# Moving one remainder's transposes from the matrix engine to DMA, four casts from ACT to GpSimd, and loading one weight in four pieces

## The chip, the cores and the metric

One core of one Trainium2 chip. The metric is the device time of one execution in microseconds (us), the median of several. The kernel before takes 534.5 us. The granted clock of PE is given as a share of full speed (1.00).

Names: PE is TensorE's matmuls, PEld its weight loads, DVE is VectorE, ACT ScalarE, POOL GpSimd, SP SyncE. A cast here is a copy from float32 to bf16.

## The reference

Eight batches of retention (attention with a decay and no softmax), whose output is the input of a mixture of four experts. The mixing weights are given, so every token goes through every expert.

```python
def _attn_ref(q, k, v):                      # q, k, v: (8, 8, 576, 64) float32
    scores = scale * np.matmul(q, k.transpose(0, 1, 3, 2))
    Dmat = np.where(rel >= 0, gamma ** rel, 0.0)
    return np.matmul(scores * Dmat, v)

def _moe_ref(x, domain_probs, w1, w2):       # x: (4608, 512), 4 experts, 1024 hidden
    p = domain_probs / (domain_probs.sum(-1, keepdims=True) + 1e-09)
    for e in range(E):
        h = np.maximum(x @ w1[e], 0.0)
        out += p[:, e:e + 1] * (h @ w2[e])
```

## The kernel before

The kernel works in bf16 through 9 token tiles of 512 tokens. Its order of instructions is fixed by hand. A batch has 576 tokens: 512 in blocks and a **remainder** of 64 whose queries go against the last 128 keys (class `Rem`). Retention work is put between expert matmuls by numbered **slots**: after each group of up or down products, `run(slots, n)` issues what hangs at slot `n`. The first token tile has slots 0 to 31, eight for each expert (four up groups, four down groups), so 16 to 19 are the up groups of the third expert (number 2) and 20 to 23 its down groups.

```python
    class Rem:
        def cast(self, engine=nc.gpsimd): ...          # k, q scaled by decays to bf16; v to bf16
        def trans_pe(self):
            pt = ring_tile("ptr", [128, 2, NP, 128], BF16)          # PSUM, one of 4 in turn
            for i, n, w in ((0, "k", 128), (1, "q", R)):
                for p in range(NP):
                    nc.tensor.transpose(pt[:, i, p, 0:w], bfr[n]..., ident[0:w, 0:w])
            nc.scalar.activation(self.kT, pt[:, 0], Copy)
            nc.scalar.activation(self.qT, pt[:, 1, :, 0:R], Copy)
        def trans_dma(self):                                        # used by later batches
            for dst, n, w in ((self.kT, "k", 128), (self.qT, "q", R)):
                nc.sync.dma_start_transpose(out=dst, in_=bfr[n]...)
        def scores(self):
            ...4 matmuls sr <- kTr, qTr
            nc.vector.tensor_tensor(self.sT, s, trir..., op=MULT)   # "the mask"
        def values(self):
            ...8 matmuls or <- sTr, bfr_v and or <- qTr, sbd; then ACT copies to xt

    def w_sum(which, lo, hi): ...      # sums of down weights, 128x1024 each, on DVE

    class Unit:                        # a quarter of batch 0 or 1 (two heads' halves)
        def cast(self, n, engine):
            if n == "v":
                if engine is nc.scalar: nc.scalar.activation(dst, self.raw["v"], Copy)
                else:                   engine.tensor_copy(dst, self.raw["v"])
                return
            engine.tensor_tensor(dst, self.raw[n], ..., op=MULT)

    load_w1_at = {1: (slice(0, F // 4),), 2: (slice(F // 4, F // 2), slice(F // 2, F))}
    ...
    load_w1(2); load_w2(2); load_v(0); load_v(1); load_w1(3); load_v(2); load_w2(3)  # GpSimd's DMA queue
    ...
    remainder(slots, 0, (-1, 13, 15, 16, 17))    # cast 13, transposes 15, scores 16, values 17
    def v_cast(u):
        vs[u].cast("k", nc.vector); vs[u].cast("q", nc.vector); vs[u].cast("v", nc.scalar)
        ...
    # for units 0 to 3 of batch 1: slots of cast, transposes, scores, values
    for u, (c, tr, sc, o) in enumerate(((17, 20, 22, 23), (19, 22, 24, 25), (24, 0, 28, 29), (25, 0, 29, 30))): ...
    for j, ats in enumerate(((18, 18, 19, 20), (20, 21, 23, 23), (28, 28, 29, 29), (30, 30, 40, 41))): ...  # w_sum
```

Each engine works through its own list in order: where DVE's list says "cast unit 0's k, then ..., then the mask", a late k holds up the mask.

## Time and profile before

| | before |
|---|---|
| time, first series | 534.53 us (534.08 to 535.23, 6 runs) |
| span of the profiled run, mean granted clock | 533.0 us, 0.999 |
| PE busy, PE instructions | 523.9 us (98%), 4220 |

This is DVE's timeline of the kernel before (columns: start, length, engine, line, operation, output<-inputs, shapes, count, and in brackets the idle time before it with what ended it):

```profile
48.41 0.42 DVE L338 TENSOR_TENSOR sTr<-sr,trir 128x256 bf16<-128x256 f32 x1 [0.98 <-PE sr L337]
49.82 0.69 DVE L529 TENSOR_TENSOR bf_k<-raw_k,gk 128x512 bf16<-128x512 f32 x1 [0.99 <-DMA raw_k<-in_k_dram]
...
57.72 1.41 DVE L409 SCALAR_TENSOR_TENSOR acc<-po,pm,acc 128x512 f32<-128x512 f32 x2 [1.78 <-PE po L397]
```

`sTr` is the mask of the remainder: it comes ahead of the casts of batch 1's unit 0, which wait for a DMA until 49.82. `acc` is the accumulation that empties a PSUM buffer; DVE is 1.78 us early for it.

### The profile page before, as it was taken

Reading aid. Unit: us, or ns where it says so; the run is one execution under the profiler, and the core shown is the slowest. Engines: PE = TensorE matmul, PEld = TensorE weight load, DVE = VectorE, ACT = ScalarE, POOL = GpSimd, SP = SyncE. Lnnn points to the kernel's source line nnn. Section 1 sums busy time; section 2 is a strip of 40 time slices with the busy share of each in tenths; the row PEclk is TensorE's granted clock in tenths of the full one; section 3 lists DMA queues with packets and bytes.
Section 4 is the critical chain, followed back from the end, with each engine's and each line's share of the span. In section 5 each row is a group of like instructions: output and inputs, shape, how many; then the busy total and the mean of one; then the engine's idle time right before and its main releaser. Section 6 shows DMA issues by size and latency. Waiting matters only on the chain.

```text
span 533.0 us, 10194 instructions
## 1 busy us (share of the span) xinstructions
PE 523.9 (98%) x4220; PEld 342.1 (64%) x4259; DVE 361.4 (68%) x458; ACT 85.2 (16%) x173; POOL 147.8 (28%) x191
## 2 busy tenths in 40 slices
PE   8999999999999999999999999999999999999997
PEld 4644544478745885478646865587548844884486
DVE  6436768895577667697678757776765567557763
ACT  4723440012101111020101101110110000000010
POOL 5744104245244434235232604053000000000000
PEclk9999999999999999999999999999999999999999
DMA  9999947878769866837363675454011111110001
GB/s 242 187 216 245 249 131 189 171 153 170 174 147 154 165 140 152 161 77 171 98 137 92 147 134 115 104 122 123 20 41 29 52 39 41 41 42 19 1 24 56
DMA packets 145054, 63.55 MB, mean 119 GB/s; under 512 B 123760, under 2 KB 135808, under 8 KB 145008
## 3 DMA queue, kind: packets, MB, share of 16 engines
q1 hardware_dynamic: 134080, 43.42, 36.8%
q0 software_dynamic: 10784, 19.35, 16.9%
q8 instruction: 33, 0.54, 0.4%
q10 hardware_dynamic: 144, 0.13, 0.1%
q14 instruction: 13, 0.11, 0.1%
HBM read 53.56 MB, written 9.51 MB: 118 GB/s over the span
## 4 chain that ended last, share of the span: by engine, by line
PE 73%; ACT 2%; issue 0%; DVE 0%
PE ph L358 36%; PE pd L474 34%; ACT xt L291 2%; PE o L283 1%; PE o L278 1%; PE py L474 1%; DVE h L364 0%; PE or L343 0%; PE sr L337 0%; PE or L345 0%; DVE ob L502 0%
## 5 line engine op out<-in xcount | busy, mean ns | idle before, releaser
L358 PE MATMUL ph<-xt,w 128*128 128x512 bf16 x1102 | 248.8, 379 | 2.5 <-DVE h L364 0.2
L364 DVE SCALAR_TENSOR_TENSOR h<-ph,pB 128x1024 bf16<-128x1024 f32 x128 | 156.5, 1224 | 57.5 <-PE ph L358 56.6
L358 PEld LDWEIGHTS <-w 128*128 128x128 bf16 x1136 | 109.9, 98 | 127.9
L474 PEld LDWEIGHTS <-h 128*128 128x128 bf16 x1024 | 99.9, 98 | 13.4
L474 PEld LDWEIGHTS <-s 128*128 128x128 bf16 x768 | 75.0, 98 | 8.7
L474 PE MATMUL pd<-wx,h 128*128 128x256 bf16 x512 | 61.1, 273 | 0.2
L474 PE MATMUL pd<-wx,s 128*128 128x256 bf16 x512 | 61.1, 273 | 0.0
L219 POOL DMA_DIRECT2D pB<-pd x28 | 15.8, 565 | 151.3 <-DVE h L364 151.3
L509 POOL TENSOR_TENSOR ob<-v,p 128x256 f32<-128x256 f32 x15 | 11.3, 756 | 115.8 <-DVE v L506 86.4
L238 POOL TENSOR_TENSOR bf_k<-raw_k,gk 128x512 bf16<-128x512 f32 x24 | 26.6, 1108 | 35.0 <-DMA raw_k<-in_k_dram 17.1
L270 DVE TENSOR_TENSOR sT<-s,tri 128x1024 bf16<-128x1024 f32 x24 | 28.3, 1219 | 6.4 <-PE s L268 6.4
L291 ACT ACTIVATE xt<-o 128x768 bf16<-128x768 f32 (+6 forms) x24 | 13.0, 594 | 116.8 <-PE o L283 116.8
L447 DVE TENSOR_TENSOR s<-s,h 128x1024 bf16<-128x1024 bf16 x32 | 31.5, 1024 | 0.0
L474 PE MATMUL pd<-t4w,h 128*128 128x256 bf16 x256 | 30.6, 273 | 0.0
L397 PE MATMUL po<-wx,h 128*128 128x512 bf16 x124 | 28.6, 379 | 0.3 <-issue 0.2
L474 PE MATMUL pd<-t3w,h 128*128 128x256 bf16 x240 | 28.7, 273 | 0.0
L474 PE MATMUL pd<-t2w,s 128*128 128x256 bf16 x240 | 28.7, 273 | 0.0
L482 ACT ACTIVATE p<-pd 128x256 f32<-128x256 f32 x16 | 6.1, 384 | 138.5 <-PE pd L474 112.8
L238 POOL TENSOR_TENSOR bf_q<-raw_q,gq 128x512 bf16<-128x512 f32 x24 | 27.3, 1138 | 1.9 <-DMA raw_q<-in_q_dram 1.8
L451 DVE TENSOR_TENSOR s<-h,s 128x1024 bf16<-128x1024 bf16 x32 | 24.3, 799 | 0.0
L445 DVE TENSOR_TENSOR s<-h 128x1024 bf16<-128x1024 bf16 x32 | 24.1, 794 | 0.0
L491 DVE TENSOR_TENSOR u<-pd,p 128x256 f32<-128x256 f32 x15 | 6.4, 425 | 22.9 <-PE pd L474 22.9
(161 smaller groups left out, 375.5 us busy)
## 6 DMA issues: line engine op xcount, KB each, us to landing
pB<-pd POOLq DMA_DIRECT2D x28, 256.0 KB, 3.7
raw_k<-in_k_dram SPq DMA_DIRECT2D x48, 128.0 KB, 2.7
raw_q<-in_q_dram SPq DMA_DIRECT2D x48, 128.0 KB, 2.9
raw_v<-in_v_dram SPq DMA_DIRECT2D x48, 128.0 KB, 3.0
out_dram<-oa SPq DMA_DIRECT2D x16, 256.0 KB, 2.4
out_dram<-ob SPq DMA_DIRECT2D x15, 256.0 KB, 2.2
w<-in_moe_w_dram POOLq DMA_DIRECT2D x3, 1024.0 KB, 14.0
wx<-in_moe_w_dram POOLq DMA_DIRECT2D x3, 1024.0 KB, 14.9
```

The lines of the kernel that those rows point to most:

```text
L219: eng.dma_start(out=pB[t, e], in_=pd[e:e + 1, t * NT:(t + 1) * NT].to_broadcast([128, NT]))
L238: eng.tensor_tensor(bfs[p % 2][n], raw1[n], g[:, :, 2 * p:2 * p + 2].unsqueeze(3).to_broadcast([128, NC, 2, D]), op=MULT)
L270: nc.vector.tensor_tensor(sT[:, :, :, :].rearrange("p j c t -> p (j c) t"), s[:, :, :, :].rearrange("p j c t -> p (j c) t"), tri[:, :].uns ...
L291: nc.scalar.activation(xt_of(t)[:, self.ps, n0 + a - t * NT:n0 + z - t * NT], o[:, :, a:z], Copy)
L358: nc.tensor.matmul(ph[:, f, :], lhsT=w1_sb[e][:, dc, fc * 128:(fc + 1) * 128], rhs=x[:, dc, :], start=(dc == 0), stop=(dc == NDC - 1))
L364: nc.vector.scalar_tensor_tensor(h[:, fk:fk + 2, :], ph, 0.0, pB[t, e][:, :].unsqueeze(1).to_broadcast([128, 2, NT]), op0=MAX, op1=MULT)
L397: nc.tensor.matmul(po[:, gg, :], lhsT=h[:, e * NFC + fc, (2 * m + gg) * 128:(2 * m + gg + 1) * 128], rhs=wx[e // 2][:, (e % 2) * NFC + fc, ...
L445: nc.vector.tensor_tensor(self.alloc("s1")[:, l], h[:, l, self.b], h[:, r, self.b], op=ADD)
L447: nc.vector.tensor_tensor(self.alloc("s2")[:, l], self.s1[:, l], h[:, l, self.a], op=SUB)
L451: nc.vector.tensor_tensor(self.alloc("s4")[:, l], h[:, r, self.a], self.s2[:, l], op=SUB)
L474: mm = nc.tensor.matmul(dst, lhsT=src[:, kk, tok], rhs=rhs(c), start=(start and c == 0), stop=(c == KH - 1), skip_group_check=True)
L509: nc.gpsimd.tensor_tensor(self.ob[:, HF:Dm], self.v, self.p5, op=ADD)
```

## The change

Intent: give PE's eight transposes of batch 0's remainder to DMA, whose result is needed only some 13 us after the remainder's inputs are there; take four casts from ACT; and let the first expert's last up weights arrive in smaller pieces. To give the DMA transposes time, the remainder's products move from slots 16 and 17 to 19 and 20, and the casts of units 0 and 1 one slot on. That puts the mask behind unit 0's casts and two weight sums in DVE's list.

```diff
-        def trans_pe(self): ...              # the eight transposes on PE and two copies on ACT
         def cast(self, n, engine):
             if n == "v":
-                if engine is nc.scalar:
-                    nc.scalar.activation(dst, self.raw["v"], Copy)
-                else:
-                    engine.tensor_copy(dst, self.raw["v"])
+                engine.tensor_copy(dst, self.raw["v"])
                 return
-    load_w1_at = {1: (slice(0, F // 4),), 2: (slice(F // 4, F // 2), slice(F // 2, F))}
+    load_w1_at = {1: (slice(0, F // 4),), 2: (slice(F // 4, F // 2), slice(F // 2, 3 * F // 4)),
+                  3: (slice(3 * F // 4, F),)}
-    remainder(slots, 0, (-1, 13, 15, 16, 17))
+    rem0 = Rem(0)
+    for at, f in ((11, lambda: rem0.cast(nc.vector)), (11, rem0.trans_dma), (19, rem0.scores), (20, rem0.values)):
+        add(at, f)
     def v_cast(u):
-        vs[u].cast("v", nc.scalar)
+        vs[u].cast("v", nc.gpsimd)
-    for u, (c, tr, sc, o) in enumerate(((17, 20, 22, 23), (19, 22, 24, 25), (24, 0, 28, 29), (25, 0, 29, 30))):
+    for u, (c, tr, sc, o) in enumerate(((18, 21, 22, 23), (20, 22, 24, 25), (24, 0, 28, 29), (25, 0, 29, 30))):
```

More of the change, by code (lines that the diff above doesn't have):

```diff
@@ L316, in alloc_trans @@
             self.qT = atp.tile([128, NP, R], BF16, tag="qTr", name="qTr", bufs=1)
-        def trans_pe(self):
-            self.alloc_trans()
-            pt = ring_tile("ptr", [128, 2, NP, 128], BF16)
-            for i, n, w in ((0, "k", 128), (1, "q", R)):
-                for p in range(NP):
-                    nc.tensor.transpose(pt[:, i, p, 0:w], bfr[n][0:w, p, :, :].rearrange("p j d -> p (j d)"),
-                                        ident[0:w, 0:w])
-            nc.scalar.activation(self.kT, pt[:, 0], Copy)
-            nc.scalar.activation(self.qT, pt[:, 1, :, 0:R], Copy)
         def trans_dma(self):
@@ L746 @@
     load_w2(3)
-    def remainder(slots, b, at):
-        add = lambda i, f: slots.setdefault(i, []).append(f)
-        x = Rem(b)
-        l, c, tr, s, o = at
-        if b > 0:
-            add(l, lambda: load_rem(b))
-        add(c, lambda: x.cast(nc.vector))
-        add(tr, x.trans_pe)
-        add(s, x.scores)
-        add(o, x.values)
     def run(slots, i):
```

## The prediction

> **What bounds the kernel now.** I read the busy shares first, then the chain that ended last, then busy time by stretch, then the matrix engine's timeline where the change works.
>
> ```profile
> PE 523.9 (98%) x4220; PEld 342.1 (64%) x4259; DVE 361.4 (68%) x458; ACT 85.2 (16%) x173; POOL 147.8 (28%) x191
> PE 73%; ACT 2%; issue 0%; DVE 0%
> ```
>
> TensorE is busy 98% of the span and carries the chain; ACT, which the change unloads, has 16%. A busy matmul row is no proof by itself, because neighbouring matmuls overlap. So I cut the first token tile, where the whole change lies, into stretches (columns: length, then busy time and count of PE, weight loads, DVE, ACT, POOL, then granted clock, DMA share, GB/s):
>
> ```profile
> 0.00:17.00 17.00, 14.86 (x206) 8.59 (x207) 10.63 (x23) 8.76 (x16) 10.58 (x21) 1.00 1.01 226
> 17.00:25.00 8.00, 7.82 (x79) 5.34 (x73) 2.81 (x19) 5.88 (x13) 7.03 (x17) 1.00 1.19 189
> 25.00:45.60 20.60, 20.50 (x96) 9.20 (x96) 7.64 (x17) 5.12 (x5) 8.21 (x11) 1.00 1.17 210
> 45.60:63.00 17.40, 17.30 (x141) 8.74 (x142) 11.66 (x19) 9.09 (x13) 5.40 (x7) 1.00 1.12 259
> 63.00:83.00 20.00, 19.47 (x199) 9.69 (x199) 15.35 (x25) 9.21 (x24) 0.00 (x0) 1.00 0.69 173
> ```
>
> In the first 17 us PE lacks 2.14 us, while inputs arrive. After that it lacks 0.18, 0.10, 0.10 and 0.53 us: 0.9 us of 66. Nor are the matmuls waiting inside their records: 32 products of expert 1 run from 38.91 to 45.81, that is 0.216 us each, and 8 up products from 46.35 to 48.09 give 0.217. PE is issue-bound from about 19 us to the end. Work taken off PE therefore shortens the run one for one; work taken off another engine is worth nothing unless PE waited for it.
>
> **The operation that goes.** PE's timeline around the remainder of batch 0 (columns: start, length, engine, line, what):
>
> ```profile
> 38.91 7.07 PE L397 MATMUL po<-wx,h 128*128 128x512 bf16 x31
> 45.81 0.39 PE L323 MATMUL ptr<-ident,bfr_k 128*128 128x128 bf16 x4
> 46.13 0.29 PE L323 MATMUL ptr<-ident,bfr_q 64*128 64x64 bf16 x4
> 46.35 1.90 PE L358 MATMUL ph<-xt,w 128*128 128x512 bf16 x8
> 48.09 0.28 PE L337 MATMUL sr<-qTr,kTr 128*128 128x64 bf16 x4
> ```
>
> Records overlap, so I take starts: transposes begin at 45.81, the next product at 46.35. They hold PE for 0.54 us, or 68 ns each. The Trainium skill, page "TensorE: Matmul & The Clock Gate", section "Part 4: PE-mode transpose", gives about 390 ns for one alone and 275 ns within a kernel; this trace has a record of 219 ns for a k transpose, but a cost in the stream of only 68 ns. Pricing 8 by the record would promise 1.7 us; the stream can give back 0.54.
>
> **Part 1: remainder of batch 0.** PE loses the 8 transposes: -0.54 us. Its 4 score products (0.11 us, 48.09 to the next start at 48.20) and 8 value products stay and move from inside the third expert's up products to its end and to after the first group of its down products. ACT loses two copies out of PSUM (0.60 and 0.38 us), DVE keeps its three casts but does them about 6 us earlier, and SyncE gains two DMA transposes. These must land before PE reaches the scores. That time is 45.81 plus 4 groups of 1.73, or 52.73.
>
> Will they? The remainder's inputs land at 36.9 to 38.8 (issue times plus time to landing: last k 23.78 + 14.0, q 26.93 + 11.9). k is cast by about 38.6, q by 39.5 (0.69 us each). The transposes are issued at about 38.7 and 40.0 (1.2 us an issue in this trace). Now they meet the weight stream:
>
> ```profile
> pd<-pn SPq DMA_DIRECT2D x1, 72.0 KB, 10.0
> kTr<-bfr_k SPq DMA_TRANSPOSE x7, 4.0
> qTr<-bfr_q SPq DMA_TRANSPOSE x7, 2.4
> q0 software_dynamic: 208, 0.35, 94.7%
> q1 hardware_dynamic: 207, 0.03, 17.7%
> ```
>
> The first three lines are issues with their median time to landing; the last two are packets of the two queues in 40 to 42 us. A transpose takes 2.4 to 4 us in the quieter later stages. But the mixing weights' 72 KB, issued at 34.93 on the same queue, took 10.0 us, and all of its packets moved between 38.5 and 44.7. The page "DMA: Bandwidth & Descriptors", section "Queues, rings and completion order", says each DMA engine takes turns between queues packet by packet; 208 against 207 agrees. So SyncE's queue gets about 104 packets/us here. Two transposes have 539 packets at 68.4 to 70.5 where about one k-sized one moved, so k has about 512 and q half, 256. Behind the 512 of the mixing weights, 768 packets at 104/us start at 44.6 and end near 52; where the weight packets are larger (48 to 50: 201 in 2 us) it is slower, where they are smaller (44.7 to 48: 618 in 3.3 us) faster. My estimate is landing at 51 to 53 against a need at 52.73. This is the one real danger in the change: probably in time, by under 1 us.
>
> **Part 2: v casts of batch 1 to GpSimd.** ACT loses 4 casts of 0.63 us. No PE wait names them in the trace, and ACT had 8 us free of the 17.4 us from 45.6 to 63, so this gains nothing directly. GpSimd gains 4 of about 0.61 us (as its casts at the start). In its order they stand behind the DMA issues that end near 52.8, so unit 0's v is ready near 53.5, unit 1's near 56; their first readers on PE come near 59 and 65. What they can hurt is DVE:
>
> ```profile
> 53.92 0.68 DVE L422 TENSOR_TENSOR t2w<-wx,wx 128x1024 bf16<-128x1024 bf16 x1
> 99.95 1.06 POOL L238 TENSOR_TENSOR bf_q<-raw_q,gq 128x512 bf16<-128x512 f32 x1
> 99.95 2.16 DVE L422 TENSOR_TENSOR t2w<-wx,wx 128x1024 bf16<-128x1024 bf16 x1
> ```
>
> The same weight sum takes 0.68 us alone and 2.16 beside GpSimd's casts. The page "SBUF — State Buffer", section "Who interferes with whom", says why: a DVE instruction with two SBUF inputs and a GpSimd instruction that reads SBUF exclude each other. The trace agrees. Each new cast can cost DVE up to 0.6 us. DVE's closest duty is the mask after the remainder's scores: scores end near 52.9, the mask takes 0.42, values need it at 54.56 (8 products of 0.216 later). In front of it stand two casts and two weight sums, 2.8 us of work from about 50 to 52.8 with DMA waits between; slack about 1.2 us, or 0.6 with a collision. Next, the accumulation after the third expert's first pair had 1.78 us of idle ahead of it and loses 0.42 to the mask and 0.6 to a collision: still fits. Cost to PE: 0.
>
> **Part 3: four pieces of w1.** The 512 KB piece issued at 12.98 landed 8.0 us later, at 21.0; its first half is wanted at 21.65. PE did not wait. With quarters, the third lands earlier, the fourth is wanted only 1.73 us later: 0 us gained, some slack gained. One more GpSimd issue (0.75 us) pushes what follows, among it the first down weights (landed 23.5, wanted 25.09; second half 26.1 against 26.8). DMA is saturated from 9 us (share over 1), so landings follow bytes queued, not issue times: 0, at worst 0.3.
>
> **Sum.** -0.54 (transposes) + 0 + 0, plus an expected 0.1 for the late-transpose risk: 534.54 - 0.54 + 0.1 = 534.1.
>
> **The rivals.** (a) *The DMA transposes land late* and PE stands before the remainder's scores: a stand of 0.3 to 2 us, time 534.3 to 536. For: the 10 us of the mixing weights, saturated DMA. Against: 12 to 14 us are allowed, and the packet count ends just inside. I give it 3 in 10. (b) *DVE becomes the wait* through GpSimd's casts, at the mask or at the accumulation that frees PSUM: 534.2 to 535. For: 2.16 against 0.68. Against: over 1 us of slack at each duty. 1 in 10. (c) *Freed ACT and earlier weights speed up the start*: up to 0.5 us more, 533.5. For: 2.1 us of PE's idle time lies in the first 17 us. Against: there PE waits on input loads and short chains that the change does not touch, and ACT's casts lie after 51 us. 1 in 10.
>
> **Range and chances.** Three runs of the kernel before spread over 1.15 us, so a median carries some 0.4 us either way; with (a) upward and (c) downward I take 533.3 to 535.2. Two per cent is 10.7 us; all rivals together do not reach it. Faster 0.01, same 0.98, slower 0.01.
>
> **What would show it.** Right: the eight transposes are gone from PE, the first up product of the third expert follows the second expert's last down product without a gap, near 45.8, and everything after, including the end, stands about half a microsecond earlier. In the list of waits, no PE or weight-load wait for the two transposes, for a v cast on GpSimd, or for the mask. Time to landing of the two new transposes near 10 us. Rival (a) shows as weight loads of the remainder's scores waiting for a DMA; (b) as value or later products waiting for DVE; (c) as an earlier first up product of expert 0 at 21.65. The prediction is wrong if the end moves by more than 1 us, or if PE's busy time does not fall by what eight transposes cost.

## The result, and the profile after

The changed kernel takes 534.0 us (533.73 to 534.68, 6 runs), the kernel before 534.53. All outputs are right. Ratios here are the mean time of one kernel's runs over that of the other's of the same rounds, so not quite the ratio of the medians quoted: 0.999, 95% interval 0.9978 to 1.0003. The same, as predicted, and within 0.1 us of the predicted time; how much of that nearness is luck is said further down.

The page of the changed kernel has eight PE instructions fewer. Its line of busy times (busy, share of the span, count), and the stretch in which the change works:

```profile
PE 523.0 (98%) x4212; PEld 341.4 (64%) x4251; DVE 363.1 (68%) x458; ACT 82.4 (15%) x167; POOL 151.8 (28%) x196
```

```profile
45.60:63.00 17.40, 16.92 (x133) 8.41 (x133) 11.72 (x19) 6.65 (x9) 7.09 (x9) 1.00 1.11 249
```

PE's busy time fell, and yet in this stretch PE now lacks 17.40 - 16.92 = 0.48 us where it lacked 0.10. PE's timeline of the changed kernel shows both sides:

```profile
39.09 7.07 PE L387 MATMUL po<-wx,h 128*128 128x512 bf16 x31
45.99 7.07 PE L348 MATMUL ph<-xt,w 128*128 128x512 bf16 x32
52.90 0.28 PE L327 MATMUL sr<-qTr,kTr 128*128 128x64 bf16 x4
...
55.28 0.19 PE L333 MATMUL or<-sTr,bfr_v 128*128 128x64 bf16 x1 [0.37 <-DVE sTr L328]
```

The second expert's down products run into the third's up products at 45.99 with no transposes between, and the scores start at 52.90 without a wait for the DMA transposes. But at 55.28 the first value product has waited for the mask. DVE's timeline of the same profile says why:

```profile
51.97 0.69 DVE L516 TENSOR_TENSOR bf_k<-raw_k,gk 128x512 bf16<-128x512 f32 x1 [4.36 <-DMA raw_k<-in_k_dram]
...
53.48 0.69 DVE L408 TENSOR_TENSOR t3w<-wx,wx 128x1024 bf16<-128x1024 bf16 x1
54.20 0.69 DVE L410 TENSOR_TENSOR wx<-wx 128x1024 bf16<-128x1024 bf16 x1
54.81 0.42 DVE L328 TENSOR_TENSOR sTr<-sr,trir 128x256 bf16<-128x256 f32 x1
```

The cast of k starts at 51.97 where it started at 49.82: the load came late, and the mask is fifth in that list: cast of k, cast of q, two weight sums (`t3w`, `wx`), mask. Each weight sum here took its normal 0.69 us, so GpSimd was not in the way yet (beside its casts a weight sum takes longer, as the prediction shows; I call that the lock).

Spans of single executions differ by tenths from how the first inputs arrive. So I compare the stream of work: the start of one and the same instruction in both profiles, this kernel minus the kernel before, at three places: the first relu (about 20 us, before the transposes, the moved casts and the moved slots), the relu at 65 us (behind it), and the last output (530 us). The difference between the first and the others is what the change gained or lost on the path. All numbers in us:

| profile | at 20 us | at 65 us | at 530 us | cast of unit 0's k |
|---|---|---|---|---|
| before | 0 | 0 | 0 | 49.82 |
| changed | +0.18 | +0.17 | +0.12 | 51.97 |
| changed, 2nd (`e0_after_again`) | -0.10 | -0.65 | -0.61 | 50.86 |
| changed, 3rd (`e11_after_third`) | -0.02 | -0.02 | -0.08 | 51.79 |

In the first profile the transposes' 0.55 us is gained and given back within 10 us. The experiments ask what gives it back, and how often.

### The profile page after: what moved, and what is told of

Its sections match the earlier page's. It is cut to its first block, busy times and chain, and to the rows that moved or that the text cites. A ratio compares the mean times of both kernels' runs of the same rounds, so it can differ in the third digit from the quotient of the medians.

```text
span 532.9 us, 10183 instructions
## 1 busy us (share of the span) xinstructions
PE 523.0 (98%) x4212; PEld 341.4 (64%) x4251; DVE 363.1 (68%) x458; ACT 82.4 (15%) x167; POOL 151.8 (28%) x196
## 4 chain that ended last, share of the span: by engine, by line
PE 73%; ACT 2%; issue 0%; DVE 0%
PE ph L348 36%; PE pd L464 34%; ACT xt L291 2%; PE o L283 1%; PE o L278 1%; PE py L464 1%; DVE h L354 0%; PE or L333 0%; PE or L335 0%; PE sr L327 0%; DVE ob L492 0%
```

## The experiments

Each is a build of the changed kernel with one edit, unless it says "kernel before". "Before" in brackets is the kernel before on the same chip in the same rounds.

### The changed kernel again, twice

> The changed kernel once more, for a second profile and more times. Theory T (the queue): the two DMA transposes slow the saturated weight queue, unit 0's inputs of batch 1 land near 52 to 54 us instead of 49.8 to 51.6, so the two casts and two weight sums that stand before the remainder's mask on VectorE end late, and the matrix engine waits 0.3 to 0.6 us before the remainder's first value product. T expects that wait again in this profile, at the same place, with 534.0 +- 0.4. Rival (one-off): the wait in the first profile belonged to an unlucky start of that run; it is under 0.1 us here.

534.24 us (533.77 to 536.1, 6 runs) [534.73], ratio 0.9996 (0.9984 to 1.0008). Its PE timeline, then DVE's:

```profile
54.46 0.19 PE L333 MATMUL or<-sTr,bfr_v 128*128 128x64 bf16 x1
```

```profile
50.86 0.69 DVE L516 TENSOR_TENSOR bf_k<-raw_k,gk 128x512 bf16<-128x512 f32 x1 [3.53 <-DMA raw_k<-in_k_dram]
...
53.70 0.42 DVE L328 TENSOR_TENSOR sTr<-sr,trir 128x256 bf16<-128x256 f32 x1
```

Here k came 1.1 us earlier than in the first profile, the mask was done at 54.12, and the value products began at 54.46 without a wait: the whole 0.55 us is kept (-0.10 to -0.65). The wait that my theory expected here did not come; the rival's figure, under 0.1 us, did. It takes the third profile to decide.

> The changed kernel a third time, as a measure of how much its result moves from one profile to the next, and beside the version above on the same chip. Theory: 0 to 0.6 us under the kernel before, and in the profile either a wait of up to 0.6 us before the remainder's first value product with unit 0's k cast after 51.5 us, or none with k cast before 51.2 us.

534.45 us (533.82 to 535.02, 5 runs) [534.77], ratio 0.9993 (0.9981 to 1.0006). k was cast at 51.79, and the first value product, at 55.09, had again waited for the mask. So the changed kernel has two outcomes: gain kept, or gain given back.

The three profiles give the condition. Where nothing but the list delays it, the first value product can start 3.31 us after the cast of k starts (51.97 to 55.28 in the first, 51.79 to 55.09 in the third). PE wants it at 54.46 in the second, whose stream started 0.10 early; so at 54.56 for a stream on time. The break-even for the cast of k is 54.56 - 3.31 = 51.25, shifted by the stream's start. The third: 51.79 - (51.25 - 0.02) = 0.56 late, and it lost 0.55. (The 3.31 is taken from these same profiles; the run with three pieces, below, repeats it.)

### Transposes back on PE, all else as changed

```diff
+        def trans_pe(self): ...      # as in the kernel before
-(11, rem0.trans_dma), (19, rem0.scores), (20, rem0.values)
+(15, rem0.trans_pe), (19, rem0.scores), (20, rem0.values)
```

> Changed kernel with the remainder of batch 0 transposed on the matrix engine again, all else (later products, early casts, v casts on GpSimd, four pieces) as changed. T expects: +0.54 us of matrix-engine work; the second down weights and unit 0's inputs land 1 to 1.5 us earlier than in the changed kernel (inputs k near 50.5, q near 51.4); the wait before the value products gone or under 0.1 us; so the stream after that place stands within 0.15 us of the changed kernel's and the time is the same within 0.3 us. Rival (four pieces or GpSimd cause the late landing): the inputs land as late as in the changed kernel, the wait of 0.5 us stays, and the time is 0.5 us above the changed kernel.

534.92 us (534.67 to 535.28, 5 runs) [534.73], ratio 1.0004 (0.9991 to 1.0017). Its PE timeline, then a line of DVE's:

```profile
46.00 0.39 PE L323 MATMUL ptr<-ident,bfr_k 128*128 128x128 bf16 x4
...
46.54 7.08 PE L358 MATMUL ph<-xt,w 128*128 128x512 bf16 x32
```

```profile
49.96 0.69 DVE L526 TENSOR_TENSOR bf_k<-raw_k,gk 128x512 bf16<-128x512 f32 x1 [2.34 <-DMA raw_k<-in_k_dram]
```

The stream started at +0.19, like the first profile's +0.18, and stood at +0.19 at 65 us: 0.54 us of transposes paid, no wait at the mask. Now k was cast at 49.96, 2.0 us earlier than in the changed kernel at the same start, although the v casts, the four weight pieces and the slots are all as changed. So the DMA transposes, and nothing else in the change, make unit 0's loads late. The other profiles agree: with the stream's start taken out, k is cast at 49.8 in this one and in the kernel before, and at 51.0 to 52.2 in the six profiles that have DMA transposes, the loads in their order and k's cast ahead of the mask. The time was expected within 0.3 us of the changed kernel's and was missed: it is 0.7 us over its 534.24 of the same rounds, whose profile had kept the gain.

How, the two queues show. These are the packets, megabytes and share of the 16 engines' time from 45.0 to 51.7 us, first of this run, then of the changed kernel (`q0` is GpSimd's queue with weights and unit loads, `q1` SyncE's with the transposes):

```profile
q0 software_dynamic: 929, 1.88, 112.3%
```

```profile
q0 software_dynamic: 872, 1.33, 96.6%
q1 hardware_dynamic: 730, 0.17, 21.0%
```

The transposes move almost nothing, 0.17 MB, but in 730 packets that take 21% of 6.7 us, 1.4 us. GpSimd's queue moved 0.55 MB less, which at its 1.88 MB in 6.7 us is 2.0 us of work: the 2.0 us by which k is late. (The kernel before moved 1.88 MB there too.) As an estimate of the size this is rough: in the second profile the queue moved 1.38 MB, which makes 1.8 us, and k was late by only 1.2 us, starts taken out.

### Ten sets of transposes on PE (kernel before)

```diff
-            for i, n, w in ((0, "k", 128), (1, "q", R)):
+            for i, n, w in ((0, "k", 128), (1, "q", R)) * 10:
```

> The kernel before with the remainder's eight matrix-engine transposes done ten times over (same result, the copies are overwritten). It measures what eight of them cost in the stream. My step: 0.54 us for eight, so nine more sets cost 4.9 us, time near 539.6. Rival (the record's length is the cost, 0.20 us each): 9 times 1.6 = 14.8 us, near 549.5. Rival (hidden beside other work): near 534.7.

539.56 us (539.43 to 539.78, 4 runs) [534.92], ratio 1.0086 (1.0073 to 1.0099). Its PE timeline, with the first two sets' k transposes and the first up product after the last set:

```profile
45.87 0.39 PE L323 MATMUL ptr<-ident,bfr_k 128*128 128x128 bf16 x4
...
46.41 0.40 PE L323 MATMUL ptr<-ident,bfr_k 128*128 128x128 bf16 x4
...
51.36 1.90 PE L358 MATMUL ph<-xt,w 128*128 128x512 bf16 x8
```

The sets stand 0.54 us apart; nine more moved the stream by 4.95 us (+0.06 to +5.01): 0.55 us a set, 69 ns a transpose on average (k's at 128x128 more, q's at 64x64 less). This is the price that the prediction read off the starts, 0.54 us and 68 ns.

### The mask ahead of the weight sums

```diff
-((18, 18, 19, 20), (20, 21, 23, 23),
+((19, 19, 19, 20), (20, 21, 23, 23),
```

> Changed kernel with the first two weight sums moved behind the remainder's mask on VectorE; same work. T expects the wait of 0.5 us before the value products to be gone and the matrix engine's stream to stand about 0.5 us earlier after it, of which up to 0.3 us may come back as a wait of the second unit's transposes for the PSUM buffer that the accumulation frees (it ended at 60.25 in the first profile, and would now be wanted at about 60.0): time 0.2 to 0.5 us below the changed kernel of the same rounds. Rival (GpSimd's casts lock VectorE): the sums are not the cause, the wait stays at 0.3 us or more.

534.61 us (534.42 to 535.59, 5 runs) [534.73], ratio 1.0001 (0.9989 to 1.0013). With two sums fewer in front, the mask ran at 54.01 although k came as late as 52.50, and PE did not wait there. But the delay came out one duty later. PE's timeline:

```profile
61.42 0.38 PE L527 MATMUL pt<-ident,bf_k 128*128 128x128 bf16 x4 [1.23 <-DVE acc L399]
```

and DVE's:

```profile
58.49 1.55 DVE L408 TENSOR_TENSOR t3w<-wx,wx 128x1024 bf16<-128x1024 bf16 x1
```

The time was expected 0.2 to 0.5 us below the changed kernel's of the same rounds and came 0.4 us above. Unit 1's transposes need the PSUM buffer that the accumulation empties; it began at 59.97 instead of 57.72. One weight sum beside a GpSimd cast took 1.55 instead of 0.68. Stream: +0.33 to +1.08. So the 1.78 us of idle ahead of the accumulation were used up by late loads (k 2.68 us later than before), the mask's new place (0.33) and the lock (0.87 in this sum, 0.3 in an earlier one) together; by this reckoning most of the 1.23 us would not have been waited without the lock.

### Two more orders for DVE

```diff
-enumerate(((18, 21, 22, 23), ... ((18, 18, 19, 20), (20, 21, 23, 23),
+enumerate(((19, 21, 22, 23), ... ((19, 19, 24, 24), (26, 26, 27, 27),
```

> A try at a version that keeps the gain whatever the start: changed kernel with unit 0's k and q casts and the first two weight sums behind the remainder's mask on VectorE, and the next six weight sums moved on by 4 to 6 groups, into the fourth expert, where VectorE has room. Theory Q expects no matrix-engine wait over 0.1 us at the mask nor at the second unit's transposes, with a late start too: the stream after 63 us stands 0.5 us ahead of the kernel before when both are reckoned from the first up product, time 533.9 to 534.2, spread of the runs smaller than the changed kernel's (533.7 to 536.1). Rival: VectorE is the wait there whatever the order; a wait of 0.3 us or more shows up elsewhere, for instance at the later units.

535.18 us (534.72 to 535.98, 5 runs) [534.92], ratio 1.0004 (0.9992 to 1.0016). The mask now stands ahead of unit 0's casts, and the gain passes 65 us whole: +0.16 to -0.39. Then 0.64 us go (+0.25 at 121 us). Its waits for PE between 60 and 85 us (total, times, longest) name the place:

```profile
PE o L608 <- DVE sT L552: 0.7, 1, 0.7
```

Four sums at slots 26 and 27 stand in DVE's list before the masks (`sT`) of units 2 and 3, and what the list is behind by reaches the value products. I tried once more, with the second four sums in the next token tile:

```diff
-enumerate(((18, 21, 22, 23), ... ((18, 18, 19, 20), (20, 21, 23, 23),
+enumerate(((19, 21, 22, 23), ... ((19, 19, 23, 23), (36, 36, 37, 38),
```

> The changed kernel with the mask ahead of unit 0's casts (they move from slot 18 to 19) and the first eight weight sums taken apart: two at slot 19, two at slot 23, and the second four at slots 36 to 38, in the next token tile, where DVE is freer. Theory: no wait at the remainder's values, none at the accumulation, none at the masks of units 2 and 3 (which cost the version with four sums at slots 26 and 27 0.64 us), so the whole 0.55 us of the transposes is kept to the end: 533.9 to 534.2 us where the kernel before takes 534.5 to 534.8. Rival (some other engine or the start takes it back anyway): within 0.2 us of the kernel before, with a new wait in the list.

534.7 us (534.47 to 535.13, 5 runs) [534.77], ratio 1.0 (0.9987 to 1.0012). No wait through the whole first tile: +0.01 to -0.54, the full gain, with k cast behind the mask. It was lost in two later places. DVE's timeline, then two lines of PE's:

```profile
99.55 2.98 DVE L412 TENSOR_TENSOR t2w<-wx,wx 128x1024 bf16<-128x1024 bf16 x1
```

```profile
108.84 3.61 PE L348 MATMUL ph<-xt,w 128*128 128x512 bf16 x15 [0.73 <-DVE h L354]
...
172.29 0.28 PE L327 MATMUL sr<-qTr,kTr 128*128 128x64 bf16 x4 [0.38 <-DMA qTr<-bfr_q]
```

The sums at slots 36 to 38 met GpSimd's casts (2.98 us for a sum of 0.68), DVE's relus fell behind, and PE waited: 0.58 us. At 172 us a later batch's remainder waited for its own DMA transpose: another 0.48 us. The second wait is not of this edit: the run with three pieces, below, has it too (0.47 at 173.05), the second profile of the changed kernel has not. Expectation missed: in neither of these two orders do the sums cost nothing. I found no version that beats both kernels.

### The products back in their old slots, transposes by DMA

```diff
-(19, rem0.scores), (20, rem0.values)
+(16, rem0.scores), (17, rem0.values)
```

> Changed kernel with the remainder's score and value products back inside the third expert's up products (where they stood before), but still fed by the DMA transposes. My reading is that the move is what hides the transposes: q's lands near 51.7, the scores would be reached at about 47.8, so the matrix engine waits about 3.9 us for the DMA and the time is 3.3 to 4.2 us above the changed kernel, near 537.9. Rival (the transposes would have been in time anyway; the move only costs): same time as the changed kernel or 0.5 us below it.

537.67 us (536.78 to 538.27, 4 runs) [534.73], ratio 1.0053 (1.004 to 1.0066). PE's timeline:

```profile
50.41 0.28 PE L327 MATMUL sr<-qTr,kTr 128*128 128x64 bf16 x4 [2.98 <-DMA qTr<-bfr_q]
```

Without the later slots PE waits 3 us for the transposes. Moving the products is what hides them, and it is also what put the mask behind unit 0's casts: the part that saves the change is the part that exposes it.

### v casts back on ACT

```diff
-        vs[u].cast("v", nc.gpsimd)
+        vs[u].cast("v", nc.scalar)
```

> Changed kernel with batch 1's v casts on ScalarE again, the rest as changed. Two profiles of the changed kernel differ: in one the matrix engine waited 0.53 us before the value products (its input loads came 0.2 us late at the start, unit 0's k was cast at 51.97), in the other (50.86) it did not wait at all, and the mask-first run waited 1.23 us for the accumulation that frees the PSUM buffer, with a weight sum stretched to 1.55 us beside a GpSimd cast. Theory Q (late loads, not GpSimd): with a normal start the time is the changed kernel's within 0.2 us, the weight sums last 0.7 us each instead of 1.0 to 1.5, and where the start is late the wait at the mask (not the one at the accumulation) is still there. Rival (GpSimd's casts are what costs): 0.3 to 0.6 us faster than the changed kernel's 534.2.

535.1 us (534.54 to 538.11, 6 runs) [534.92], ratio 1.0012 (0.9994 to 1.0031). Expectation missed: it should have been within 0.2 us of the changed kernel's 534.24. The stream went from -0.01 to +0.11 at 65 us and +0.76 by 74 us. ACT's timeline, then PE's waits from 45 to 75 us:

```profile
53.18 0.63 ACT L515 ACTIVATE bf_v<-raw_v 128x512 bf16<-128x512 f32 x1 [0.97 <-DMA raw_v<-in_v_dram]
53.71 1.01 ACT L352 ACTIVATE h<-ph 128x1024 bf16<-128x1024 f32 x1
```

```profile
PEld L387 <- ACT h L352: 2.3, 3, 1.0
```

On ACT the cast of v waits for its late load, and the relu behind it waits too; the down products need that relu. This happens twice: here, and with a later unit's v, cast at 71.21. The weight sums between 52 and 62 us all took 0.68 or 0.69 us in this run, so the longer ones of the other runs come from GpSimd's casts. So with DMA transposes the move of the v casts to GpSimd is worth up to 1.3 us to the path (-0.55 wanted, +0.76 found), though the medians show less of it: 0.2 us over the kernel before, where the changed kernel has 0.3 to 0.5 us under it. One of the six executions took 538.11 at a mean granted clock of 0.996, the others at most 535.78. One profile is one sample; the mechanism is shown, its usual size is not.

### Three pieces

```diff
-2: (slice(F // 4, F // 2), slice(F // 2, 3 * F // 4)), 3: (slice(3 * F // 4, F),)
+2: (slice(F // 4, F // 2), slice(F // 2, F))
```

> Changed kernel with expert 0's up weights in three pieces again. My reading: no effect, because the weight queue is saturated; third piece lands near 21, first product of it starts without a wait at about 21.6, unit 0's k is cast at 50.5 to 52 as in the changed kernel, time within 0.3 us of 534.2. Rival (the fourth piece is what makes the later loads late): unit 0's k is cast about 1 us earlier than in the changed kernel with the same start, near 50.

534.69 us (534.07 to 535.82, 4 runs) [534.92], ratio 0.9997 (0.9984 to 1.001). The profiled run started late (+0.24). From 20 to 66 us PEld has one wait for a weight:

```profile
PEld L348 <- DMA w<-in_moe_w_dram: 0.2, 1, 0.2
```

It stands at 32.13 and is for the second expert's up weights, which neither kernel cuts into pieces; it moved the stream by about 0.06 us (+0.24 to +0.30). The large piece's first products came at 21.88 without a wait. So in this profile the fourth piece is worth nothing, and k is not cast earlier without it, which was the rival. The rest of that profile is the story told already: k cast at 52.30, a wait for the mask until 55.61, which is 52.30 + 3.31.

### Unit 0's loads made late, in both kernels

```diff
-    load_v(0)
-    load_v(1)
+    load_v(1)
+    load_v(0)
```

> The changed kernel with the loads of batch 1's units 0 and 1 in the other order, so that unit 0's k, q and v land about 2.7 us later than in the changed kernel (k near 54.6 us). Theory (what takes the gain back is that unit 0's loads are late, and its casts stand on DVE in front of the remainder's mask): DVE's casts of k and q, the two weight sums and the mask slide by the same 2.7 us, and PE waits before the remainder's first value product for 2.5 to 3.5 us; the stream ends 2 to 3 us behind the kernel before, some 536.5 to 537.5 us. Rival (GpSimd's casts in DVE's way are what costs; late loads are harmless): no wait longer than 1 us there, time within 0.7 us of the changed kernel.

539.16 us (538.13 to 539.76, 4 runs) [534.77], ratio 1.0085 (1.007 to 1.0101): even more than expected. PE's timeline:

```profile
57.24 0.21 PE L333 MATMUL or<-sTr,bfr_v 128*128 128x64 bf16 x1 [2.40 <-DVE sTr L328]
...
57.64 3.23 PE L387 MATMUL po<-wx,h 128*128 128x512 bf16 x8
```

The cast of k started at 53.64. The first value product was wanted at 54.56 + 0.12 = 54.68 and came at 57.24: 2.56 us, inside the expected 2.5 to 3.5, although k was cast 1 us earlier than expected; about 0.3 of it is the lock (the second weight sum took 0.98). The rest was not expected. The eight down products after the pause took 60.71 (the next start) - 57.64 = 3.07 us, not the usual 8 times 0.216 = 1.73: 1.34 us more. Busy time in that stretch (columns as in the prediction; the third figure from the end is the granted clock):

```profile
57.20:60.50 3.30, 3.26 (x16) 1.42 (x16) 3.30 (x5) 0.38 (x1) 1.93 (x3) 0.52 1.11 265
```

After PE stood for some 2.4 us its clock was granted at 0.52 for 3.3 us; the next stretch has 1.00. The Trainium skill, page "TensorE: Matmul & The Clock Gate", section "What's actually happening", describes this: half rate after an idle window of about 3.4 us, full rate after a busy one, with a window that runs free of the kernel. The trace agrees on the half rate and on about the length of the slow stretch. But it drops after a pause shorter than one window, while the profile of the version with the products in their old slots stood about 3 us and kept 1.00. That version's other executions help: its four took 536.78 and 537.12 at a mean granted clock of 0.999 and 1.000, and 538.22 and 538.27 at 0.997. One build, run four times, seems to have lost some 1.3 us to the clock in two of them. That where the pause falls in a free-running window decides would fit, but no run here tests it.

> The kernel before with the same exchange of the two loads: its mask is done before unit 0's casts, so the theory expects no wait at the remainder's value products although k lands near 52.5 us and is cast 2.7 us later. What it may cost: up to 0.8 us for a relu on ACT that stands behind the cast of unit 0's v (which lands near 54.3 us, the wait that the run with v cast on ACT showed), or a little at the accumulation. Total 0 to 0.8 us over the kernel before. The rival (late loads cost wherever they stand) expects 2 to 3 us here too.

536.65 us (535.88 to 537.6, 4 runs) [534.77], ratio 1.0036 (1.0022 to 1.0049): 1.9 us more, where up to 0.8 was expected. k was cast at 52.89, later than in the changed kernel's first profile, and there is no wait at the remainder's values, whose mask was done at 49.05. As expected the wait is for a relu behind the cast of v on ACT, but it is longer and comes twice (1.12 and 0.31 us). PE's timeline of the first:

```profile
55.99 0.60 PE L397 MATMUL po<-wx,h 128*128 128x512 bf16 x2 [1.12 <-ACT h L362]
```

The stream went from +0.22 to +2.00. So late loads do cost wherever an in-order engine has a needed result behind them: DVE's mask in the changed kernel, ACT's relu in the kernel before. What the rival said of DVE ("late loads are harmless") falls; what it said of both kernels ("late loads cost wherever they stand") is nearer the truth than my theory.

## Why the prediction was right, point by point

**PE's price of the transposes: right.** 0.54 us from starts, not 1.7 from records; 0.55 us a set when multiplied, 0.54 when put back, 0.55 kept in the second profile of the changed kernel.

**Landing of the DMA transposes: right, a little pessimistic.** Estimated 51 to 53 us against a need at 52.73. The q transpose landed at 51.69, 50.55 and 51.39 in the three profiles, for scores that started at 52.90, 52.62 and 52.70: in time by 1.2 to 2.1 us, not "by under 1 us". The two transposes moved 832 packets (1360 on SyncE's queue from 38 to 54 us, 528 of them in the kernel before too), where 768 were reckoned. Rival (a) did not happen; the 0.1 us charged for it was for the wrong risk.

**Slack at the mask, "about 1.2 us": mis-sized.** This is the term that failed. It took the casts and sums in front of the mask "from about 50 to 52.8", that is with the loads at their times of the kernel before (k cast at 49.82). With the new packets k was cast at 51.97, 50.86 and 51.79, and the slack was -0.54, +0.29 and -0.56 us by the break-even above. The prediction had the cause in hand: it used the packet-by-packet turns of the two queues (shown again above as 872 against 730) to estimate when the transposes land, and did not ask what the other queue loses by the same turns. Some 830 packets on a DMA that is full are paid by whatever is queued beside them, here 1.2 to 2.0 us for unit 0's k.

**Rival (b), DVE as the wait at the mask, given 1 in 10: it happened in two of three profiles**, at the place named, but not by GpSimd's lock: in the first profile every instruction ahead of the mask had its normal 0.69 or 0.42 us. There the lock shows only behind the mask (0.97 and 1.09 us for a sum of 0.68; 1.55 with the mask ahead of the sums), where it helps to exhaust the accumulation's slack. The 1.78 us of idle ahead of the accumulation, which "still fits" in the prediction, were gone in the changed kernel's first profile (it began at 58.85, with no idle), though no wait followed.

**Rival (c), an earlier start: not seen.** At 20 us the three profiles stood at +0.18, -0.10 and -0.02.

**Part 2, "this gains nothing": right for the kernel before's loads, wrong in combination.** With the loads late, the cast of v on ACT would have held up a relu (`e4_v_on_act`, and the same in the kernel before when its loads were made late). GpSimd had units 0's and 1's v ready at 55.6 and 59.4, later than the 53.5 and 56 reckoned, but still ahead of its first readers at 59.85 and 65.43.

**Part 3, 0 us: right.** With three pieces PE did not wait for the large one.

**The sum.** 534.1 was predicted. The three series of the changed kernel gave 534.0, 534.24 and 534.45, against 534.53, 534.73 and 534.77 of the kernel before: 0.5, 0.5 and 0.3 us less. The gain of 0.55 us is real on PE, is kept or given back by how the loads fall in one execution, and what is left is below what the interval of any one series can separate from nothing: all three reach 1. Taken together, weighted by their scatter, the three series give 0.4 us, give or take 0.3 (my estimate of a 95% interval). The nearness of 534.0 to 534.1 is partly luck: the sum left out the giving back of up to 0.55 us, charged 0.1 us for a risk that did not come, and the result depends on how many executions kept the gain.

What stays open: how often the gain is kept. Only three executions of the changed kernel have a profile, and the first of them was the slowest of its six (534.68; the others 533.73 to 534.38). What makes unit 0's k earlier in one execution was not tested. The record has a hint: the earlier the remainder's own k is cast on DVE (37.40 in the second profile; 38.80 and 38.64 in the first and third), the earlier SyncE issues its transpose (38.12; 39.52 and 39.36) and the earlier unit 0's k comes. It may be that the transposes' packets are then sooner done, or that all loads are earlier alike.

## What to carry to other kernels

When work goes to DMA, price it twice: when it lands, and what it takes from transfers already queued; on the full DMA here, small packets cost more than their bytes: 0.17 MB of them came with 0.55 MB less on the other queue. Then follow the late transfers into each in-order engine and look at what stands behind their first reader: a result needed soon must not stand behind a load that may come late. A gain of half a microsecond on the bounding engine is only worth what the next tightest slack lets through, so measure that slack with the change in place.

## What the Trainium skill lacked or had wrong

- Page "TensorE: Matmul & The Clock Gate", section "Part 4: PE-mode transpose": its 390 ns alone and about 275 ns in a kernel are lengths of one instruction (219 ns here for 128x128); the cost in the stream is not given. It was 69 ns here on average (72 more transposes: 4.95 us), from the starts about 80 ns for one of 128x128 and 55 ns for one of 64x64, and that is the figure a change gains or loses.
- The same page, section "What's actually happening": a pause of about 2.4 us was followed by 3.3 us at a granted clock of 0.52, so a pause need not be as long as the idle window of about 3.4 us that the page asks for; a pause of about 3 us in another profile was followed by a clock of 1.00.
- Page "DMA: Bandwidth & Descriptors", section "Queues, rings and completion order": turn-taking by packets agrees (208 against 207 in the prediction's window), but the section does not say what it costs the other queue. Here 730 small packets with 0.17 MB took 21% of the engines' time over 6.7 us, and the weight queue moved 1.33 instead of 1.88 MB.
